# An attention and expert kernel: counts two places behind their comparisons, a step budget for routing, and query and value loads in exchanged places

## The chip, the cores and the metric

The program runs on one core of a Trainium2 chip. The metric is the device time of one execution in microseconds (us); lower is better. Engines are called as in the profile: PE (TensorE), DVE (VectorE), ACT (ScalarE), POOL (GpSimd) and SP (SyncE, which here only issues transfers).

## What is computed

Attention over 4 batches of 8 heads, 768 positions of 64 numbers, in which a position sees the first 8 positions and the last 96, with a bias that falls with distance. Its output, 3072 tokens of 512 numbers, goes to a mixture of 8 experts: each token goes to its best expert, and each expert keeps the 80 tokens with the largest gate.

```python
scores = scale * np.matmul(q, k.transpose(0, 1, 3, 2)) + bias
a = softmax(where(keep, scores, -1e9)); attn = np.matmul(a, v)
x = attn.transpose(0, 2, 1, 3).reshape(B * S, H * D)
expert_idx = np.argmax(x @ w_gate, axis=1)
for e in range(E):
    tok_idx = the (at most 80) tokens of expert e with the largest gate
    out[tok_idx] = gate_w[tok_idx, None] * (np.maximum(x[tok_idx] @ w1[e], 0) @ w2[e])
```

## The kernel before

**Rounds.** The attention runs in 24 rounds (t = 0 to 23), one block of 128 queries with all 8 heads in each; a round has two units a_ = 2t and b_ = 2t + 1 of four heads. What stands in a round is written out by hand and every engine runs its instructions in that order. A round holds work of several blocks: the second half of the values' products of block t-3 (`own`, L321), the scores of block t (`scores`, L173), the softmax of its two units (`soft`: L190 on DVE, L194 on ACT), the transposes of the probabilities of block t-1 (`transposes`, L227 to L240 on PE; one half of the result is copied by ACT, L244, the other by DVE in `copied`, L250), the first half of the values' products of block t-2 (`common`, L306), the division of the probabilities by their sums (`norm`: L201 and L202 on DVE, then L207 on POOL), and small products for the gate (`logits1`, `logits2`). The transposes write to PSUM tiles that must have been copied out before the next transposes start.

**Routing.** Blocks are gathered in groups of 6, 6, 6, 4 and 2. When the gate's numbers of a group are there, the choice of experts runs as a Python generator whose steps, one or two instructions each, are strewn into later rounds: `routes(4)` stands in the middle of a round (behind the transposes of unit b_ - 2 and ahead of their DVE copy), `routes(5)` at its end. I call these the middle and the end place. For a group of six the steps are: seven for the largest gate (`all`), for the first group alone those of a scale, then `choose` with its comparisons (L582, one per block, 127 columns each, on DVE), two empty steps, `count` (L639: six pairs of a weight load and a small matmul on PE that read the comparisons), one more empty step, and then the finish: the capacity's subtraction (L573), two steps on `re` (L599, L600), two for the gate (L608, L609) and eight on POOL (`columns`, L619 to L626). An empty step costs one of the four or five and nothing else. The first three groups finish inside the rounds, so their counts stand at the end of rounds 11, 16 and 22.

**Loads.** SP issues all transfers in one order. In a round it stores two pieces of attention output (L253; each waits for the DVE copy of its unit), loads the values of block t+1 and a piece of the next batch's keys behind the first store, and the queries of block t+2 and, in some rounds, 512 KB of expert weights (L90) or of zeros (L94) behind the second. Each transfer also waits for the one eight places ahead of it. Queries and values have four buffers each. The values of a block are first read two rounds after its scores.

**Behind the rounds** come a drain, in which the last units and the last two groups follow a written order (`DRAIN`, where `r` is one routing step), the search for each expert's threshold, and the experts.

Of the kernel before, what the change touches and what calls it, by code (L numbers as in the profile page):

```python
# [15 lines left out]
ALU = mybir.AluOpType  # L16
# [8 lines left out]
NT = B * NB  # L25
# [35 lines left out]
STAY = (3, 0)  # L61
SPLIT = (4, 4, 4)
FAR = 1.0e6
END = object()
SLOPES = [2.0 ** -(h + 1) for h in range(H)]


def fast_path(tc, a, out, cst, x_dram, inp):
    nc = tc.nc
    V, A, G, T = nc.vector, nc.scalar, nc.gpsimd, nc.tensor  # L70
    ident = cst["ident"]

    with ExitStack() as ctx:
# [63 lines left out]
        with tc.tile_pool(name="at_sb", bufs=2) as sp, ExitStack() as sctx:  # L137
# [255 lines left out]
                for _ in islice(g, n):  # L393
                    pass

            def routes(n):
                for _ in range(n):
                    while routing and next(routing[0], END) is END:
                        routing.pop(0)

            routing, cst["later"], cst["landed"] = [], [], []
            nu = 2 * NT
# [8 lines left out]
            for t in range(NT):  # L411
                a_, b_ = 2 * t, 2 * t + 1
                if t % NB == 1 and t // NB + 1 < B:
                    keys = inp.keys(t // NB + 1)
                if t == 0:
                    for _ in cst["first"]:
                        pass
                begin(a_)
                begin(b_)
                if 3 <= t:  # L420
                    own(t - 3)
                scores(a_)
                scores(b_)
                if t:
                    norm(b_ - 2)
                soft(a_, (0,))
                if t:
                    transposes(a_ - 2)
                soft(a_, (1,))
                soft(b_, (0,))  # L430
                if t:
                    copied(a_ - 2)
                if 2 <= t < NT - 1:
                    inp.load_v(t + 1)
                keys = keys if keys and next(keys, END) is not END else None
                soft(b_, (1,))
                if t % 2 == 0 and 4 <= t:
                    logits1(t - 4, 2)
                if t % 2 and 5 <= t:
                    logits2(t - 5, 2)  # L440
                norm(a_)
                if t == 0:
                    for _ in window:
                        pass
                    for z in pwz:
                        G.memset(z[:, 4 * WH:], 0.0)
                    G.memset(cst["zero"], 0.0)
                if t:
                    for _ in range(6):
                        next(late, None)  # L450
                if 2 <= t:
                    common(t - 2)
                if t:
                    transposes(b_ - 2)
                routes(4)
                if t:
                    copied(b_ - 2)
                if 1 <= t < NT - 2:
                    inp.load_q(t + 2)
                for k in ASKS[t]:  # L460
                    next(dict(w=ahead, o=wipe).get(k, iter(())), None)
                routes(5)
# [29 lines left out]
            go(choice, 99)  # L492
            cn = lps[:, 3 * P + 2 * E:3 * P + 3 * E]
            count(nc, cn, [rt])
            routes(99)
            assert not routing
            go(end, 1)
            gs1 = cst["gs1"]
# [14 lines left out]
class Route:  # L513
# [36 lines left out]
    def scale(self, ps):  # L550

        V, n, scl = self.nc.vector, self.n, self.cst["scl"]
        c = 1.0 / (STEPS * n * P)
# [1 line left out]
        mb = self.sp.tile([P, 1], BF16, name="mb", bufs=1)  # L555
        yield V.tensor_reduce(out=ms, in_=self.sx, axis=AX.X, op=ALU.add)
        yield V.tensor_scalar(out=mb, in0=ms, scalar1=-c, scalar2=float(E) * n * c, op0=ALU.mult, op1=ALU.add)
        yield
        yield
        self.nc.tensor.matmul(ps, self.cst["ones"], mb, start=True, stop=True, skip_group_check=True)  # L560
        yield V.tensor_scalar(out=scl[:, 0:1], in0=ps, scalar1=1.0 / 32, scalar2=None, op0=ALU.mult)
        kv = self.cst["kval1"]
# [2 lines left out]

    def rest(self, cn, capm):
        yield from self.choose()
        yield
        yield
        count(self.nc, cn, [self])  # L570
        if capm is not None:
            yield
            yield self.nc.vector.tensor_tensor(out=capm[:P - 1], in0=capm[:P - 1], in1=cn[:P - 1], op=ALU.subtract)  # L573
        yield from self.finish()

    def choose(self):
# [13 lines left out]
        if self.ones:  # L590
            yield V.tensor_reduce(out=self.m2, in_=eq, axis=AX.X, op=ALU.max)
        yield V.tensor_tensor(out=oh, in0=eq, in1=self.wide(self.m2), op=ALU.is_equal)
        m = 1 if self.t0 + n < NT - 5 else 2
        for t in range(n - 1 if self.ones else 0, n, m):
            yield compare(t, min(m, n - t))

    def finish(self):
        V, re = self.nc.vector, self.re
# [13 lines left out]
    def columns(self):  # L612


        G, oh, n = self.nc.gpsimd, self.oh, self.n
        c = [self.bx[:, :, i, :] for i in range(6)]
        og = self.cst["og"][:, self.t0:self.t0 + n]
        tv = self.cst["tval"][:, self.t0:self.t0 + n]
        yield G.tensor_tensor(out=og, in0=oh, in1=self.wide(self.gate), op=ALU.mult)  # L619
        yield G.tensor_copy(out=c[3], in_=og)  # L620
        yield G.tensor_tensor(out=c[0], in0=oh, in1=self.wide(tv), op=ALU.mult)
        yield G.tensor_tensor(out=og, in0=og, in1=c[3], op=ALU.subtract)
        yield G.tensor_copy(out=c[4], in_=og)
        yield G.tensor_tensor(out=c[1], in0=oh, in1=self.cst["pval"].unsqueeze(1).broadcast_to([P, n, E]), op=ALU.mult)
        yield G.tensor_tensor(out=c[5], in0=og, in1=c[4], op=ALU.subtract)
        yield G.tensor_copy(out=c[2], in_=oh)  # L626


# [812 lines left out]
```

## Time and profile before

| | us |
|---|---|
| median of three runs | 284.09 |
| lowest and highest of them | 281.59, 286.69 |
| the profiled execution's own time | 282.35 |
| its span from first to last instruction | 280.5 |
| of the span: the 24 rounds up to the last scores' start | 146 |
| the drain and the search | 146 to 178 |
| the experts | 178 to 280.5 |

Busy shares over the whole span are PE 89%, DVE 81%, ACT 73%, POOL 48%. A busy share averages over stages, so the rounds are read one by one in the timeline: which engine's row has an idle time in brackets, and what ended it.

### The profile page before, as it was taken

To read this page: it belongs to the slowest core of one execution; us is meant where nothing else is said; L and a number is where in the kernel's file an instruction comes from. 1 tells how busy PE (TensorE), PEld (TensorE's weight loads), DVE (VectorE), ACT (ScalarE), POOL (GpSimd) and SP (SyncE) were. 2 spreads that over 40 slices of the span, in tenths; PEclk is the share of its full clock that TensorE was granted. 3 is DMA by queue.
4 is the path that set the end of the run, shared out by engine and by line. 5 is a ranking of instruction groups with operands and counts; after the bars stand their busy time and mean duration, and the time that the engine had idled before them with its cause. 6 is when DMAs were issued, how large, how long until landed. Compare 5 with 4: busy or idle time off the path is not lost. (4 is left out here: it accounts for less than half of the span.)

```text
span 280.5 us, 9657 instructions
## 1 busy us (share of the span) xinstructions
PE 248.6 (89%) x3585; PEld 184.2 (66%) x3585; DVE 227.9 (81%) x785; ACT 204.6 (73%) x583; POOL 134.2 (48%) x203
## 2 busy tenths in 40 slices
PE   6769989997995969979878988999999999999990
PEld 2457868875884859767767774556666666666660
DVE  4968768899676887937966777989999999999960
ACT  4888879986686757857856455678798887989730
POOL 7585656443373242734334143880826537173431
PEclk9999999999899888979989975999999999999997
DMA  6999999967779799999861069799999999990001
GB/s 175 315 275 362 271 285 318 329 202 221 201 212 293 208 308 370 301 345 303 237 230 48 17 231 361 238 316 333 398 395 381 397 315 403 349 370 24 23 27 29
DMA packets 48030, 73.06 MB, mean 260 GB/s; under 512 B 3656, under 2 KB 22472, under 8 KB 47976
## 3 DMA queue, kind: packets, MB, share of 16 engines
q1 hardware_dynamic: 46808, 69.74, 76.3%
q0 software_dynamic: 1024, 2.62, 3.0%
q8 instruction: 30, 0.49, 0.7%
q14 instruction: 24, 0.20, 0.2%
q10 hardware_dynamic: 144, 0.00, 0.0%
HBM read 58.46 MB, written 13.89 MB: 258 GB/s over the span
## 5 line engine op out<-in xcount | busy, mean ns | idle before, releaser
L207 POOL TENSOR_TENSOR pwz<-pwz,z 128x672 f32<-128x672 f32 (+2 forms) x48 | 60.6, 1262 | 74.8 <-DVE z L202 22.0
L194 ACT ACTIVATE pwz<-ts,nm 128x168 f32<-128x168 f32 (+1 forms) x192 | 80.0, 420 | 20.2 <-DVE nm L190 17.6
L190 DVE CUSTOM_DVE_ANT_0 ts<-sc,tab 128x168 f32<-128x168 f32 (+1 forms) x192 | 50.6, 319 | 13.8 <-PE sc L173 13.3
L852 POOL TENSOR_TENSOR w_3l<-w,w_3h 128x1024 fp32r<-128x1024 f32 x7 | 26.8, 3828 | 37.9 <-issue 24.2
L173 PE MATMUL sc<-kt,q 64*64 64x104 f32 (+3 forms) x1088 | 37.5, 279 | 7.1 <-DMA q<-in_q_dram 6.1
L173 PEld LDWEIGHTS sc<-kt,q 64*64 64x64 f32 x1088 | 32.1, 142 | 10.7 <-DMA q<-in_q_dram 5.6
L194 ACT ACTIVATION_READ_ACCUMULATOR pwz<-ts,nm 128x1 f32 x192 | 36.3, 189 | 0.0
L250 DVE COPY ta<-tp 128x512 f32<-128x512 f32 (+2 forms) x47 | 28.6, 609 | 3.8 <-PE tp L240 2.9
L852 DVE TENSOR_TENSOR w_0l<-w,w_0h 128x1024 fp32r<-128x1024 f32 x15 | 30.3, 2019 | 1.5 <-ACT w_0h L847 1.1
L227 PE MATMUL tp<-ident,pwz 64*128 64x64 f32 x384 | 24.7, 239 | 5.7 <-ACT ta L244 2.6
L244 ACT COPY ta<-tp 128x512 f32<-128x512 f32 (+2 forms) x47 | 23.9, 508 | 5.4 <-PE tp L240 3.1
L227 PEld LDWEIGHTS tp<-ident,pwz 64*128 64x128 f32 x384 | 17.3, 141 | 14.8 <-POOL pwz L207 5.1
L306 PE MATMUL u<-ta,va 104*64 104x128 f32 (+1 forms) x352 | 25.4, 287 | 0.0
L321 PE MATMUL u<-ta,vb 64*64 64x64 f32 x608 | 24.3, 236 | 0.0
L306 PEld LDWEIGHTS u<-ta,va 104*64 104x64 f32 (+1 forms) x352 | 19.9, 142 | 6.3 <-PE tp L240 2.5
L321 PEld LDWEIGHTS u<-ta,vb 64*64 64x64 f32 x608 | 21.5, 148 | 1.3 <-issue 0.2
L852 DVE TENSOR_TENSOR w_1l<-w,w_1h 128x1024 fp32r<-128x1024 f32 x15 | 20.4, 1358 | 0.0
L921 POOL DMA_INDIRECT out_dram<-vb,si x8 | 13.8, 1720 | 12.0 <-ACT vb L920 6.8
L852 DVE TENSOR_TENSOR w_2l<-w,w_2h 128x1024 fp32r<-128x1024 f32 x15 | 18.1, 1209 | 0.0
L847 ACT CAST w_3h<-w 128x1024 fp32r<-128x1024 f32 x16 | 16.7, 1045 | 0.0
L847 ACT CAST w_2h<-w 128x1024 fp32r<-128x1024 f32 x15 | 15.8, 1056 | 1.2 <-PE hp L878 1.2
L190 DVE DVE_READ_ACCUMULATOR2_ANT nm<- 128x1 f32 x192 | 15.9, 83 | 0.0
(431 smaller groups left out, 548.0 us busy)
## 6 DMA issues: line engine op xcount, KB each, us to landing
w<-in_w_dram SPq DMA_DIRECT2D x64, 512.0 KB
out_dram<-zero SPq DMA_DIRECT2D x12, 512.0 KB
q<-in_q_dram SPq DMA_DIRECT2D x23, 256.0 KB
kt<-in_kT_dram SPq DMA_DIRECT2D x20, 272.0 KB
vb<-in_vb_dram SPq DMA_DIRECT2D x20, 256.0 KB
va<-in_va_dram SPq DMA_DIRECT2D x20, 208.0 KB
x_dram<-ta SPq DMA_DIRECT2D x28, 128.0 KB
x_dram<-kt SPq DMA_DIRECT2D x6, 256.0 KB
```

The lines of the kernel that those rows point to most:

```text
L173: T.matmul(sc[64 * i:64 * i + 64, hh, pp, o:o + e - c], q[h, pr * P + 64 * i:pr * P + 64 * i + 64], kt[h, pr, c0 + c:c0 + e], start=True, ...
L190: V.tensor_tensor_reduce(out=ts[:, j, :w], in0=sc[:, hh, pp, :w], in1=cst["tab" if m else "tab0"][:, 2 * g + pp, hh, :], scale=-0.125, sca ...
L194: A.activation(out=pw[:, j, :w], in_=ts[:, j, :w], func=AF.Exp, bias=nm[:, j:j + 1], scale=-1.0, accum_out=z[:, j:j + 1],)
L207: eng.tensor_tensor(out=p, in0=p, in1=zs.unsqueeze(2).broadcast_to(list(p.shape)), op=ALU.mult)
L227: T.transpose(out=tps[i][:, 64 * j:64 * j + 64], in_=pw[hs[i], o:o + P], identity=ident[hs[i], hs[i]])
L244: A.copy(out=ta[:, 0, :n], in_=tps[0][:, :n])
L250: V.tensor_copy(out=ta[:, 1, :n], in_=tp[:, :n])
L306: T.matmul(up[64 * hh:64 * hh + 64, pr, :], va[:n, 64 * h:64 * h + 64], ta[:n, :, 64 * j:64 * j + 64], start=pr == 0, stop=not m, skip_gro ...
L321: T.matmul(up[h, pr, 64 * i:64 * i + 64], vb[h, i, pr, :], ta[h, i, 256 + 64 * pp:320 + 64 * pp], start=False, stop=True, skip_group_check ...
L847: A.copy(out=hi, in_=src)
L852: eng.tensor_tensor(out=lo, in0=src, in1=hi, op=ALU.subtract)
L921: G.indirect_dma_start(out=out[:, :], out_offset=bass.IndirectOffsetOnAxis(ap=si[:, e:e + 1], axis=0), in_=y, in_offset=None, bounds_check ...
```

## The change

Five things are edited. (1) The places' numbers become a budget: an ordinary step costs 1, a comparison costs 3 (`SLOW`), and a `HOLD` ends the place, so that the two holds ahead of a count put it two places behind the last comparison. The middle place has 5 instead of 4. (2) All comparisons take two blocks in one instruction of 254 columns; before, those of the first three groups took one of 127. (3) POOL's eight steps are put into five yields. (4) `load_q(t + 2)` moves to where `load_v(t + 1)` stood, and the reverse. (5) At the end of the drain the remaining steps run without regard to holds.

```diff
-            def routes(n):
-                for _ in range(n):
-                    while routing and next(routing[0], END) is END:
+            def routes(n, hold=True):
+                while n > 0 and routing:
+                    step = next(routing[0], END)
+                    if step is END:
                         routing.pop(0)
+                    elif step is HOLD and hold:
+                        break
+                    else:
+                        n -= 3 if step is SLOW else 1
...
-                if 2 <= t < NT - 1:
-                    inp.load_v(t + 1)
+                if 1 <= t < NT - 2:
+                    inp.load_q(t + 2)
...
-                routes(4)
+                routes(5)
                 if t:
                     copied(b_ - 2)
-                if 1 <= t < NT - 2:
-                    inp.load_q(t + 2)
+                if 2 <= t < NT - 1:
+                    inp.load_v(t + 1)
...
         yield from self.choose()
-        yield
-        yield
+        yield HOLD
+        yield HOLD
         count(self.nc, cn, [self])
         if capm is not None:
-            yield
+            yield HOLD
...
-        m = 1 if self.t0 + n < NT - 5 else 2
-        for t in range(n - 1 if self.ones else 0, n, m):
-            yield compare(t, min(m, n - t))
+        for t in range(n - 1 if self.ones else 0, n, 2):
+            compare(t, min(2, n - t))
+            yield SLOW
```

On PE, the end of round 16 in the program before: the transposes of unit 31 end with L240, then comes the count of the third group (six such pairs; one stands here), then `own` of block 14 and the scores of round 17.

```order
L240 MATMUL tp_31_2293<-ident,ut_1242 128x64
L639 LDWEIGHTS cf_2178
L639 MATMUL lps<-oh,cf_2178 127x8
...
L321 MATMUL u_2283<-ta_2094,vb_118 64x64 x8
L321 MATMUL u_2283<-ta_2147,vb_118 64x64 x8
L173 MATMUL sc_2351<-kt_113,q_110 64x104
```

The same place of the changed program, and then the end of round 17, where the count now stands (`cf` are the comparisons' results):

```order
L240 MATMUL tp_31_2289<-ident,ut_1242 128x64
L321 MATMUL u_2279<-ta_2091,vb_118 64x64 x8
L321 MATMUL u_2279<-ta_2143,vb_118 64x64 x8
L173 MATMUL sc_2338<-kt_113,q_110 64x104
...
L240 MATMUL tp_33_2430<-ident,ut_1242 128x64
L644 LDWEIGHTS cf_2175
L644 MATMUL lps<-oh,cf_2175 127x8
...
L321 MATMUL u_2420<-ta_2236,vb_119 64x64 x8
```

So the count has moved by one round, past `own` of block 14, the scores of round 17 and that round's transposes.

On DVE, the middle and end place of round 16 before, from the reciprocal of unit 32's sums to the first softmax rows of round 17:

```order
L202 RECIPROCAL z_2182<-z_2182 128x4
L582 TENSOR_TENSOR cf_2178<-sx_1599,kval_65 128x127 x4
L250 COPY ta_2294<-tp_31_2293 128x512
L582 TENSOR_TENSOR cf_2178<-sx_1599,kval_65 128x127
L573 TENSOR_TENSOR capm<-capm,lps 127x8
L201 TENSOR_SCALAR z_2185<-z_2185 128x4
L202 RECIPROCAL z_2185<-z_2185 128x4
L190 ISA ts_2329,nm_2327<-sc_2351,tab 128x168
```

and the same stretch after the change:

```order
L202 RECIPROCAL z_2179<-z_2179 128x4
L587 TENSOR_TENSOR cf_2175<-sx_1597,kval_65 128x254 x2
L250 COPY ta_2290<-tp_31_2289 128x512
L201 TENSOR_SCALAR z_2182<-z_2182 128x4
L202 RECIPROCAL z_2182<-z_2182 128x4
L190 ISA ts_2316,nm_2314<-sc_2338,tab 128x168
```

Two comparisons of two blocks stand where four and one of one block stood, and the subtraction L573 has gone to the middle place of round 18, together with the four instructions of the finish:

```order
L202 RECIPROCAL z_2461<-z_2461 128x4
L578 TENSOR_TENSOR capm<-capm,lps 127x8
L604 TENSOR_SCALAR re<-oh 128x48
L605 TENSOR_TENSOR re<-re,sx_1597 128x48
L613 TENSOR_SCALAR sx_1597<-sx_1597 128x6
L614 RECIPROCAL gate<-sx_1597 128x6
L250 COPY ta_2572<-tp_35_2571 128x512
```

On SP, round 13 before; `q_112` is the buffer of block 15's queries:

```order
L253 DMA x_dram<-ta_1847 256x1x128
L1361 DMA va<-in_va_dram 104x512
L1362 DMA vb_118<-in_vb_dram 128x512
L1346 DMA kt_114<-in_kT_dram 128x4x136
L253 DMA x_dram<-ta_1896 256x1x128
L1354 DMA q_112<-in_q_dram 128x512
L90 DMA w_0_0_1914<-in_w_dram 128x2x512
```

and after:

```order
L253 DMA x_dram<-ta_1832 256x1x128
L1359 DMA q_112<-in_q_dram 128x512
L1351 DMA kt_114<-in_kT_dram 128x4x136
L253 DMA x_dram<-ta_1880 256x1x128
L1366 DMA va<-in_va_dram 104x512
L1367 DMA vb_118<-in_vb_dram 128x512
L90 DMA w_0_0_1903<-in_w_dram 128x2x512
```

The query load stands four places earlier, behind one store instead of two. Weight loads that the diff doesn't name have moved as well: at the end of round 16 three stood in a row before, and now rounds 15, 16 and 17 have them one at a time.

## Rows read from the trace of the kernel before

**Rows 1.** Stretches: us, busy us of each engine, PE clock, DMA share, GB/s.
```profile
103.60:106.90 3.30, 3.30 (x67) 3.30 (x68) 0.50 (x4) 0.58 (x1) 1.31 (x1) 0.50 1.12 338
107.00:116.50 9.50, 9.50 (x239) 8.02 (x232) 9.28 (x49) 8.44 (x35) 4.12 (x8) 1.00 1.04 356
178.00:280.00 102.00, 95.61 (x476) 62.93 (x476) 91.74 (x88) 77.53 (x101) 47.72 (x21) 0.99 0.77 272
```

**Rows 2.** Who waited for whom: total us, times, longest us; PE.
```profile
PE sc L173 <- DMA q<-in_q_dram: 6.1, 6, 2.9
PE lps L639 <- DVE cf L582: 5.2, 8, 1.1
...
PE lps L350 <- issue: 2.1, 1, 2.1
```

**Rows 3.** Timeline, rounds 16 and 17: start, us, engine, what [idle before].
```profile
100.63 1.97 DVE L582 TENSOR_TENSOR cf<-sx,kval 128x127 bf16<-128x127 f32 x4
...
102.45 0.42 PE L639 MATMUL lps<-oh,cf 128*127 128x8 bf16 x2 [1.09 <-DVE cf L582]
102.52 0.68 DVE L250 COPY ta<-tp 128x512 f32<-128x512 f32 x1
...
103.60 1.97 PE L321 MATMUL u<-ta,vb 64*64 64x64 f32 x32
...
106.83 0.33 DVE L190 CUSTOM_DVE_ANT_0 ts<-sc,tab 128x168 f32<-128x168 f32 x1 [2.66 <-PE sc L173]
```

**Rows 4.** Timeline, the same products and scores at the full clock, rounds 18, 19.
```profile
115.52 1.15 PE L321 MATMUL u<-ta,vb 64*64 64x64 f32 x32
...
116.51 1.41 PE L173 MATMUL sc<-kt,q 64*64 64x104 f32 x48
```

**Rows 5.** Timeline, first softmax row of rounds 12 and 23.
```profile
72.75 0.29 DVE L190 CUSTOM_DVE_ANT_0 ts<-sc,tab 128x128 f32<-128x128 f32 x1 [1.85 <-PE sc L173]
...
147.73 0.29 DVE L190 CUSTOM_DVE_ANT_0 ts<-sc,tab 128x128 f32<-128x128 f32 x1 [2.34 <-PE sc L173]
```

**Rows 6.** Timeline, rounds 13 to 15: SP's issues, PE, DVE and ACT.
```profile
80.06 0.54 SPq L253 DMA_DIRECT2D x_dram<-ta  x1
80.69 1.73 SPq L1361 DMA_DIRECT2D va<-in_va_dram  x1
...
84.25 0.60 SPq L1354 DMA_DIRECT2D q<-in_q_dram  x1
...
86.02 0.29 PE L240 MATMUL tp<-ident,ut 64*128 64x64 f32 x4
...
89.21 2.04 PE L173 MATMUL sc<-kt,q 64*64 64x104 f32 x48 [2.90 <-DMA q<-in_q_dram]
90.16 0.33 DVE L190 CUSTOM_DVE_ANT_0 ts<-sc,tab 128x168 f32<-128x168 f32 x1 [2.21 <-PE sc L173]
...
92.32 0.58 ACT L244 COPY ta<-tp 128x512 f32<-128x512 f32 x1 [0.78 <-PE tp L240]
```

**Rows 7.** Timeline, scores of rounds 21 and 22.
```profile
131.30 1.43 PE L173 MATMUL sc<-kt,q 64*64 64x104 f32 x48 [0.51 <-DMA q<-in_q_dram]
...
137.28 1.46 PE L173 MATMUL sc<-kt,q 64*64 64x104 f32 x48 [0.80 <-DMA q<-in_q_dram]
```

**Rows 8.** One line's instructions: ns min/median/max, first and last start us, forms.
```profile
L582 DVE TENSOR_TENSOR cf<-sx,kval x18: 258/282/1396, 63.8 to 144.3; 128x127 bf16<-128x127 f32 x18
L582 DVE TENSOR_TENSOR cf<-tail,kval x4: 284/355/416, 157.9 to 161.1; 128x254 bf16<-128x254 f32 x2, 128x127 bf16<-128x127 f32 x2
...
L608 DVE TENSOR_SCALAR sx<-sx x3: 140/893/1156, 75.7 to 151.2; 128x6 f32<-128x6 f32 x3
```

**Rows 9.** Timeline: POOL's division in round 16, and four counts without a wait.
```profile
100.88 1.37 POOL L207 TENSOR_TENSOR pwz<-pwz,z 128x672 f32<-128x672 f32 x1 [1.91 <-DVE cf L582]
...
159.88 0.38 PE L639 MATMUL lps<-oh,cf 128*127 128x8 bf16 x4
```

**Rows 10.** Timeline, round 19: a stall on PE.
```profile
120.67 0.58 PE L350 MATMUL lps<-ident,ls 128*128 128x128 f32 x2 [2.11 <-issue]
```

More of the change, by code (lines that the diff above doesn't have):

```diff
@@ L63 @@
 FAR = 1.0e6
-END = object()
+END, HOLD, SLOW = object(), object(), object()
 SLOPES = [2.0 ** -(h + 1) for h in range(H)]
@@ L494, in fast_path @@
             count(nc, cn, [rt])
-            routes(99)
+            routes(99, False)
             assert not routing
@@ L567, in rest @@
         yield from self.choose()
-        yield
-        yield
+        yield HOLD
+        yield HOLD
         count(self.nc, cn, [self])
         if capm is not None:
-            yield
+            yield HOLD
             yield self.nc.vector.tensor_tensor(out=capm[:P - 1], in0=capm[:P - 1], in1=cn[:P - 1], op=ALU.subtract)
@@ L618, in columns @@
         tv = self.cst["tval"][:, self.t0:self.t0 + n]
-        yield G.tensor_tensor(out=og, in0=oh, in1=self.wide(self.gate), op=ALU.mult)
+        G.tensor_tensor(out=og, in0=oh, in1=self.wide(self.gate), op=ALU.mult)
         yield G.tensor_copy(out=c[3], in_=og)
-        yield G.tensor_tensor(out=c[0], in0=oh, in1=self.wide(tv), op=ALU.mult)
+        G.tensor_tensor(out=c[0], in0=oh, in1=self.wide(tv), op=ALU.mult)
         yield G.tensor_tensor(out=og, in0=og, in1=c[3], op=ALU.subtract)
-        yield G.tensor_copy(out=c[4], in_=og)
+        G.tensor_copy(out=c[4], in_=og)
         yield G.tensor_tensor(out=c[1], in0=oh, in1=self.cst["pval"].unsqueeze(1).broadcast_to([P, n, E]), op=ALU.mult)
-        yield G.tensor_tensor(out=c[5], in0=og, in1=c[4], op=ALU.subtract)
+        G.tensor_tensor(out=c[5], in0=og, in1=c[4], op=ALU.subtract)
         yield G.tensor_copy(out=c[2], in_=oh)
```

## The prediction

> **What bounds the kernel now.** I read the stretches first [rows 1]. In the experts' 102 us PE is busy for 95.6, and nothing in the change touches them, so that part stays. In an undisturbed stretch, 107.0 to 116.5, PE is busy for all 9.50 us at a granted clock of 1.00, with DVE at 9.28 and ACT at 8.44. So a round, about 6 us from one block's scores at 131.30 to the next at 137.28 [rows 7], is paced by PE, with the two others close behind. What a round can lose is therefore a wait of PE, and the list of waits names them [rows 2]: PE waited 6.1 us in six places for queries, 5.2 us in eight places for comparisons, and 2.1 us once for nothing that the profile shows.
>
> The timeline shows what such a wait really costs [rows 3]. In round 16 DVE starts the third group's comparisons at 100.63, PE stands in the count behind them, and only at 103.60 come the products of block 14. They take 1.97 us where the same 32 take 1.15 two rounds later [rows 4], because the granted clock of 103.6 to 106.9 is 0.50, the 1.2 GHz level, after PE had stood still [rows 1]. DVE meanwhile is done with the round and waits 2.66 us for the scores, until 106.83. That idle time, not PE's, is what the stall costs: DVE's next round, and ACT's behind it, start that much late. The other two counts inside the rounds show the same, 1.85 us in front of round 12's softmax and 2.34 us in front of round 23's [rows 5].
>
> The second kind is the queries of block 15 [rows 6]. SP issues their load at 84.25; PE has finished round 14 at 86.02 + 0.29 = 86.31 and waits 2.90 us, until 89.21. DVE waits 2.21 us for the scores, and ACT another 0.78 us for PE in the slow stretch that follows.
>
> **Part by part: the counts.** With the count one round later, its comparisons have been done for a whole round, so its waits go. In round 16 PE can then follow its last transposes with the products (1.15 us) and the scores (1.41 us) [rows 4], about 2.6 us, and be done by 103; DVE's copy ends at 102.52 + 0.68 = 103.20 [rows 3]. So the scores no longer end last, and DVE sets the pace: its idle time goes, 2.66 + 1.85 + 2.34 = 6.85 us. In rounds 16 and 22 one comparison (0.28) stood behind the copy; pairing takes it out of that place: 0.56. Together 7.4 us.
>
> The comparisons themselves: five or six of 0.28 us become three of at most 0.42 [rows 8]. But the longest took 1396 ns, since POOL's division, from 100.88 for 1.37 us, runs at that moment [rows 9]. If one of each pair still meets it, DVE's middle place is about as long as before (1.39 + 0.42 against 1.97), a gain of nothing; if none does, it is 1.0 us shorter in three rounds. I take nothing, as the collision came in every group. The Trainium skill, "SBUF — State Buffer", section "Who interferes with whom", says that a DVE instruction with two SBUF inputs contends with a GpSimd instruction that reads SBUF, and that whoever starts first holds the port pair for its whole instruction. The trace agrees with its 1396 ns. By that rule a longer comparison is as exposed as a short one, and the sum is the one with nothing.
>
> What the move costs: a count is six pairs, and four took 0.38 us unhindered [rows 9], so 0.57 us. In rounds 12, 17 and 23 they now lie in a round that PE paces (9.50 of 9.50): three times 0.57 is 1.7 us lost. From below nothing, should DVE pace these rounds too; I take 1.7. The finish moves a round later, its five instructions in one middle place ahead of DVE's copy. Its `sx` step took 140 ns at its shortest and 1156 where POOL ran [rows 8]; in round 13 it now stands later behind the reciprocal that releases POOL, so it probably collides. That is between 0 and 1.0 us; DVE's spare time is small, 0.22 us of 9.50 [rows 1], but the copy that it delays has the next scores of PE, 1.41 us, as cover, so I take 0.5. POOL's steps keep their number and POOL is the least busy engine [rows 1]: hidden, as long as its 1.37 us division isn't late.
>
> **The loads.** The query load of round 13 goes from behind the values, keys and second store to right behind the first store: it can issue at 80.6 rather than 84.25 [rows 6]. Before, it landed 89.21 - 84.25 = 4.96 us after its issue. SP's next issue at 80.69 was held for 1.73 us, and the query load would now meet that hold: landing between 85.6 and 87.3, against 86.31 when PE wants it. The wait of 2.90 shrinks to between 0 and 1.0, and with a wait this short the clock need not fall. Gain: 2.21 + 0.78 = 3.0 us, or 2.0 at the poor end. The waits in rounds 21 and 22 were 0.51 and 0.80 [rows 7]; earlier loads take both away, and I count the first alone, since in round 22 DVE has a group's choice to do at that moment: 0.5. The values are read two rounds after the scores, so half a round's delay lies inside about 12 us of cover (two rounds of 6 us). If that cover were gone, each late load would cost PE what the queries' did, 2 to 3 us. The single weight loads in place of three in a row, the drain's shifted steps and the last group's count behind two transposed blocks I set at nothing: they are hidden by PE's queue of products, and at most the 0.38 us of four counts comes onto the path.
>
> **The sum**: 7.4 + 3.0 + 0.5 - 1.7 - 0.5 = 8.7 us off the profiled execution's 282.35: 273.6, and I say 274. That execution lies 1.7 us below the median of 284.09; the runs' spread of 5.1 us is the size of two such stalls, so I leave the difference in the range.
>
> **The rivals.**
>
> *More*: no comparison of a pair meets POOL, and the waits of rounds 21 and 22 both count: 1.0 us in three rounds and 0.8 on top, 274 - 3.8 = 270. Against it stands that each group had one collision; for it, that fewer instructions are exposed.
>
> *The wait moves*: DVE, 9.28 us busy of 9.50 [rows 1], is late all the same, and PE now waits for its copies of the transposes instead of its comparisons. Half of the 7.4 us stays: 277.5.
>
> *The loads do nothing*: the hold of 1.73 us, not the place in the order, sets when queries land, because the transfers are full (DMA share 1.04 and 356 GB/s [rows 1]). Then 3.5 us is missing: 277.
>
> *Slower*: PE's unexplained stall in round 19, 2.11 us at 120.67 [rows 10], comes oftener. It is a wait for nothing that the profile shows, which fits a late load of PE's own instructions behind other transfers; the stretch before it moved 356 GB/s at a DMA share of 1.04. Rounds without other waits move the same bytes in less time. One such stall costs 2.1 us and a slow clock after it (1.97 for 1.15 us on each group of products), about 3 us. Three more cancel the gain, four make it slower than 284, five or six slower by 2%. The Trainium skill, "Runtime: NRT & Kernel Launch", section "Instruction fetch mechanics", says that crossing from one block of instructions to the next is mostly hidden. By that rule this rival is worth nothing; the trace has one wait that it doesn't explain.
>
> **How the numbers follow.** I give the forecast, 271.5 to 276, 0.46; more 0.11; the wait moves 0.20; the loads do nothing 0.12; slower 0.11. A measurement of this kernel tells about 2% from no change: that is 278.4 on the fast side and 289.8 on the slow. Faster by more are the forecast and "more" whole, half of the moved wait (0.10) and 0.07 of the loads: 0.74. Slower by more is 0.05 of the last rival. Within 2% is the rest, 0.21. The range is 268.5 (all of "more", and most of the 1.7 us of the counts hidden after all) to 281 (both partial rivals at once: 282.35 less 8.7 - 3.7 - 3.5); beyond it I leave the last rival and a tail of the first.
>
> **What would show it.** Right: no wait of PE for comparisons inside the rounds; DVE's idle time in front of the first softmax of rounds 12, 17 and 23 under 0.5 us; the scores of block 15 without a wait of over 1 us; the granted clock at 1.00 at the end of round 16, where it was 0.50; the experts still 102 us. The comparisons of 254 columns should show one of about 1.4 us in a group. Wrong: a wait of PE's transposes for DVE's copy of about 1 us in each of rounds 12, 17 and 23 (the wait has moved); the queries' waits still there (the loads do nothing); several waits of PE for nothing shown (slower). If the time is out by more than 5 us, the step to doubt is that DVE's idle time can be taken off whole: that nothing else than PE's count held the next round.

## The result and the profile after

| | before | changed |
|---|---|---|
| median, us | 283.91 | 273.11 |
| lowest and highest of four runs | 281.59, 286.69 | 271.25, 274.21 |
| profiled execution's own time | 282.35 | 272.51 |
| its span | 280.5 | 270.7 |
| start of the scores of round 9 | 50.33 | 50.35 |
| from there to the start of the scores of round 23 | 96.05 | 85.10 |
| from there to the end | 134.13 | 135.22 |

The changed kernel is faster: ratio 0.9639, 95% interval 0.9548 to 0.973. The prediction was 274.0 us, 268.5 to 281.0, and 8.7 us off the profiled execution; it was 9.84 off. The table shows where: rounds 9 to 22 got 10.95 us shorter and what follows 1.09 us longer. A round's length is taken here from the first score product (L173) of its block to that of the next, read from the timeline:

| round | before | changed | difference | what stood there |
|---|---|---|---|---|
| 11, 16, 22 | 8.97, 9.65, 9.10 | 6.03, 5.92, 6.36 | -9.41 | the counts |
| 12, 17 | 5.65, 5.78 | 5.82, 6.32 | +0.71 | where two of the counts went |
| 14, 15 | 7.23, 6.50 | 4.42, 6.01 | -3.30 | the queries of block 15 |
| 19 | 8.87 | 5.98 | -2.89 | the stall of [rows 10] |
| 10, 18 | 6.68, 5.37 | 8.11, 7.05 | +3.11 | new stalls, below |
| 9, 13, 20, 21 | 22.26 | 23.07 | +0.81 | |

Lines of the kernel from the counts on are five higher than before: L582 is now L587, L639 is L644, L573 is L578.

Stretches of the changed kernel, the answer to [rows 1] (us, busy us of each engine with the number of instructions, PE clock, DMA share, GB/s): all of rounds 9 to 22, the end of round 16 with round 17, and the experts. Behind them stands the first of these stretches in the kernel before.

```profile
50.35:135.45 85.10, 76.16 (x1812) 63.36 (x1810) 74.05 (x375) 69.86 (x277) 40.98 (x56) 0.98 0.96 299
97.00:106.80 9.80, 9.52 (x237) 7.80 (x233) 8.71 (x43) 8.49 (x33) 5.23 (x4) 1.00 1.05 331
165.40:267.40 102.00, 98.14 (x489) 64.10 (x487) 94.13 (x90) 77.90 (x102) 50.22 (x22) 1.00 0.77 274
```

```profile
50.33:146.38 96.05, 82.58 (x1818) 69.11 (x1817) 76.31 (x388) 70.44 (x277) 42.26 (x57) 0.92 0.87 266
```

The last of the three is 102 us long by choice. From the experts' first product (L878, now L883) to the end it is 102.52 us before and 102.35 after, so the experts take what they took.

PE does the same work (some 1,810 products) and waits less: 85.10 - 76.16 = 8.9 us idle where it was 96.05 - 82.58 = 13.5. It also needs 6.4 us less busy time, since the granted clock has a mean of 0.98 instead of 0.92. At the end of round 16 it is 1.00, where it was 0.50. The same bytes now go through in 85 us: 299 GB/s and a DMA share of 0.96 instead of 266 and 0.87.

Who waited for whom in the changed kernel, PE, the answer to [rows 2]:

```profile
PE u L306 <- issue: 3.6, 3, 1.7
PE sc L173 <- DMA q<-in_q_dram: 2.8, 5, 1.0
...
PE sc L173 <- issue: 1.6, 2, 0.9
...
PE lps L644 <- DVE oh L597: 0.4, 1, 0.4
```

No wait of PE for comparisons (`cf`) is left, queries cost 2.8 us where it was 6.1, and the first place has a wait for "issue", nothing that the profile shows. No product waits for the values, whose loads now issue later.

Timeline of rounds 16 and 17, the answer to [rows 3] (start, us, engine, what, [idle before]):

```profile
96.59 1.15 PE L321 MATMUL u<-ta,vb 64*64 64x64 f32 x32
...
96.94 1.84 DVE L587 TENSOR_TENSOR cf<-sx,kval 128x254 bf16<-128x254 f32 x2
97.20 1.31 POOL L207 TENSOR_TENSOR pwz<-pwz,z 128x672 f32<-128x672 f32 x1 [1.91 <-DVE z L202]
97.58 1.41 PE L173 MATMUL sc<-kt,q 64*64 64x104 f32 x48
98.71 0.68 DVE L250 COPY ta<-tp 128x512 f32<-128x512 f32 x1
...
99.59 0.30 DVE L190 CUSTOM_DVE_ANT_0 ts<-sc,tab 128x168 f32<-128x168 f32 x1
...
102.52 0.46 PE L644 MATMUL lps<-oh,cf 128*127 128x8 bf16 x6
...
102.91 1.15 PE L321 MATMUL u<-ta,vb 64*64 64x64 f32 x32
```

At 96.59 PE goes on with the products of block 14 at once, in 1.15 us instead of 1.97. DVE's two comparisons run beside the scores, and its first softmax row at 99.59 has no idle time in brackets, where [rows 3] had 2.66 us. The count stands at 102.52, one round later, without a wait. Rounds 12 and 23 begin on DVE in the same way, for 1.85 and 2.34 us in [rows 5]:

```profile
71.59 0.26 DVE L190 CUSTOM_DVE_ANT_0 ts<-sc,tab 128x128 f32<-128x128 f32 x1
...
136.89 0.26 DVE L190 CUSTOM_DVE_ANT_0 ts<-sc,tab 128x128 f32<-128x128 f32 x1
```

### The profile page after: what moved, and what is told of

Its sections match the earlier page's. It is cut to its first block, busy times and chain, and to the rows that moved or that the text cites. A ratio compares the mean times of both kernels' runs of the same rounds, so it can differ in the third digit from the quotient of the medians.

```text
span 270.7 us, 9646 instructions
## 1 busy us (share of the span) xinstructions
PE 243.4 (90%) x3585; PEld 179.4 (66%) x3585; DVE 226.9 (84%) x776; ACT 204.5 (76%) x583; POOL 133.7 (49%) x203
## 5 line engine op out<-in xcount | busy, mean ns | idle before, releaser
L173 PE MATMUL sc<-kt,q 64*64 64x104 f32 (+3 forms) x1088 | 36.0, 271 | 4.3 <-DMA q<-in_q_dram 2.8
L173 PEld LDWEIGHTS sc<-kt,q 64*64 64x64 f32 x1088 | 30.7, 137 | 7.7 <-issue 3.9
L306 PEld LDWEIGHTS u<-ta,va 104*64 104x64 f32 (+1 forms) x352 | 19.1, 136 | 10.6 <-issue 6.9
L321 PE MATMUL u<-ta,vb 64*64 64x64 f32 x608 | 22.2, 224 | 0.0
L321 PEld LDWEIGHTS u<-ta,vb 64*64 64x64 f32 x608 | 19.6, 137 | 1.6 <-DMA x_dram<-ta 0.6
```

What stands on the lines that cost most here:

```text
L173: T.matmul(sc[64 * i:64 * i + 64, hh, pp, o:o + e - c], q[h, pr * P + 64 * i:pr * P + 64 * i + 64], kt[h, pr, c0 + c:c0 + e], start=True, ...
L306: T.matmul(up[64 * hh:64 * hh + 64, pr, :], va[:n, 64 * h:64 * h + 64], ta[:n, :, 64 * j:64 * j + 64], start=pr == 0, stop=not m, skip_gro ...
L321: T.matmul(up[h, pr, 64 * i:64 * i + 64], vb[h, i, pr, :], ta[h, i, 256 + 64 * pp:320 + 64 * pp], start=False, stop=True, skip_group_check ...
```

## The experiments

**The loads alone.** The kernel before, with `load_q` and `load_v` exchanged.

```diff
-                if 2 <= t < NT - 1:
-                    inp.load_v(t + 1)
+                if 1 <= t < NT - 2:
+                    inp.load_q(t + 2)
...
-                if 1 <= t < NT - 2:
-                    inp.load_q(t + 2)
+                if 2 <= t < NT - 1:
+                    inp.load_v(t + 1)
```

> The kernel before with nothing but the two loads in each other's place. Theory (the wait for queries was 3.5 us of the time): PE's wait for queries in front of the scores of block 15, 2.90 us before, is under 1 us, the waits for comparisons stay as they were (5.2 us in eight places), and the time is 3 to 3.5 us below the kernel before, about 279 against 282.35 in the profiled executions. Rival (the loads do nothing, full transfers set when queries land): the sum of PE's waits for queries stays near 6 us and the time is within 1 us of before.

Measured: 278.36 us against 282.87 of the kernel before on the same chip, ratio 0.9832 (0.9769 to 0.9895), so 3.0 to 6.5 us; by the medians 4.5, more than the 3 to 3.5 expected. PE's waits in it:

```profile
PE lps L639 <- DVE cf L582: 4.8, 7, 1.1
...
PE u L306 <- issue: 1.9, 1, 1.9
PE tp L240 <- issue: 1.7, 1, 1.7
PE sc L173 <- DMA q<-in_q_dram: 1.6, 3, 1.0
```

The comparisons' waits are there as before, the queries' have gone from 6.1 to 1.6. "The loads do nothing" has fallen. The two waits for issue are new, with a third of 1.2 us that isn't shown, and that of L350 [rows 10] is gone.

**The counts alone.** The changed kernel with the two loads back in their old places (the diff above, reversed).

> The changed kernel with the two loads back where they stood; counts, budget and pairs as changed. Theory (the three stalls at the counts cost 7.4 us, and 2.2 us of it is given back): about 277 in the profiled execution; no wait of PE for comparisons in the rounds, DVE's idle time ahead of rounds 12, 17 and 23 under 0.5 us, but the wait for the queries of block 15 still 2 to 3 us. From the round lengths of the changed kernel, which show nothing given back in rounds 12 and 17, it would rather be 274 to 275. Rival (the loads did the work): 280 or more.

Measured: 275.27, ratio 0.9696 (0.9625 to 0.9768), 6.6 to 10.6 us. PE waits for no comparison, and for the queries of block 15 it does (timeline):

```profile
86.08 0.29 PE L240 MATMUL tp<-ident,ut 64*128 64x64 f32 x4
88.42 0.85 PE L173 MATMUL sc<-kt,q 64*64 64x104 f32 x23 [2.05 <-DMA q<-in_q_dram]
```

So both parts pay by themselves. Their sum, 4.5 + 7.6 = 12.1 us by the medians, is not to be told, within these intervals, from the whole change's 10.8.

**No holds.** The changed kernel in which a hold is an empty step. This takes the first group's `scale` its two holds as well, which the change had put there too.

```diff
-                    elif step is HOLD and hold:
+                    elif step is HOLD and hold is None:
```

> The changed kernel in which a hold is an ordinary empty step and ends no place; budget, pairs and loads as changed. The counts then stand at the ends of rounds 11, 16 and 22 again, where they stood before, but with one or two paired comparisons in the same round's middle place instead of four or five single ones. Theory (the place of the count is what matters): PE waits for comparisons again, 0.4 to 1.1 us in each of these rounds, and 3 to 6 us come back: 276 to 278. Rival (fewer comparisons between the transposes and the count are enough): no wait over 0.3 us and a time within 1 us of the changed kernel's 272.5.

Measured: 273.88, ratio 0.9597 (0.9507 to 0.9687), not to be told from the changed kernel. The trace shows more. Timeline at the end of round 16, PE and then DVE:

```profile
96.95 0.28 PE L644 MATMUL lps<-oh,cf 128*127 128x8 bf16 x2 [0.37 <-DVE cf L587]
98.40 0.28 PE L644 MATMUL lps<-oh,cf 128*127 128x8 bf16 x2 [1.17 <-DVE cf L587]
...
100.95 0.33 DVE L190 CUSTOM_DVE_ANT_0 ts<-sc,tab 128x168 f32<-128x168 f32 x1 [1.55 <-PE sc L173]
```

Rounds 16 and 22, with two pairs ahead of the count, have the stall back (8.65 and 9.19 us long, against 5.92 and 6.36 with holds). Round 11, with one pair, has not (6.28 against 6.03). Rounds 9 to 22 take 89.07 us, 3 to 4 more than in the changed kernel's two traces (85.10, and 85.95 below), as expected. But from round 23 to the end it takes 133.86, 1.2 to 1.4 less. So the holds are what clears rounds 16 and 22, and about a third of what the rounds gain is paid back behind them. The theory's 3 to 6 us was right for the rounds and too much for the whole.

**One block a comparison.** The changed kernel, each pair made as two.

```diff
-            compare(t, min(2, n - t))
+            for i in range(t, min(t + 2, n)):
+                compare(i, 1)
```

> The changed kernel with each comparison of two blocks made as two of one block in the same step, so that places and budget stay. Theory (pairing is worth nothing by itself, one of each group meets POOL either way): the time stays within 0.5 us of the changed kernel's 272.5 in the profiled execution, and one comparison in each group still takes about 1.4 us. Rival (the longer instructions are what makes the middle place shorter): 0.3 to 1.0 us in each of three rounds, so 273.5 to 275.5.

Measured: 273.01, ratio 0.9645 (0.9561 to 0.9729), not to be told from the changed kernel; an effect of 1 us would not show in these intervals. The profiled execution, 273.77 us, is 1.3 above the changed kernel's, which by the expectation speaks for the rival. The rounds say otherwise: rounds 12, 16 and 17 are 0.14 to 0.15 us longer than in the changed kernel's second trace (below) and round 11 not at all, while round 21 alone has 10.24 us for 6.21 in the first trace, with a wait for issue of 2.4 us in it. One comparison in each group still takes 1.40 us. So pairing shows no effect of the size of the rival's.

**What the waits for issue are.** The changed kernel stops in round 10 and again in round 18 (timeline, PE), and a transfer of the queue "instruction" runs just before the first (transfers from 58.3 to 60.1):

```profile
58.76 0.98 PE L306 MATMUL u<-ta,va 104*64 104x128 f32 x13
...
61.39 0.44 PE L306 MATMUL u<-ta,va 104*64 104x128 f32 x3 [1.66 <-issue]
...
63.88 2.52 PE L173 MATMUL sc<-kt,q 64*64 64x104 f32 x48
```

```profile
108.41 0.98 PE L306 MATMUL u<-ta,va 104*64 104x128 f32 x13 [1.53 <-issue]
```

```profile
q8 instruction: 1, 0.02, 4.4%
```

PE stops inside a row of sixteen equal products, and the scores behind run at the slow clock: 2.52 us for 1.41, and the stretches give 0.50 from 63.1 to 66.4:

```profile
63.10:66.40 3.30, 3.30 (x70) 3.11 (x68) 2.30 (x16) 1.22 (x5) 1.31 (x1) 0.50 0.79 254
```

The trace has 30 transfers of 16 KB on that queue, for some 7,270 instructions of PE, which are 28.4 times 256. The one here began at 58.70 and took 1.27 us, and PE went on 1.42 us after its end. I numbered PE's instructions from the start of the trace (weight loads, products, semaphore waits and a few others): the first one late in round 10 has number 2241, in round 18 it has 4289, and in the kernel before the stall of [rows 10] has 4545. These are 8, 16 and 17 times 256, plus 193. A third stop, 1.04 us in round 22, has 20 x 256 + 193, though the waits put it down to ACT. The Trainium skill, "Runtime: NRT & Kernel Launch", section "Instruction fetch mechanics", says that instructions are refilled in blocks of 256, 16 KiB each; the trace agrees in the size of the transfers and in the spacing of the stops. To test it, the changed kernel was run again, and then with transfers moved.

> The changed kernel as it is, as the base of the three others of this batch. Expected 271 to 274. If PE's waits for nothing shown are late loads of its own instructions, they stand at the same places of PE's instruction stream as before: counting weight loads, matmuls and semaphore waits from the start of the trace, after a multiple of 256 plus 193, so that the 1.66 us in round 10 comes again at instruction 2241; if they are something else, they stand anywhere.

Measured: 270.95, ratio 0.9628 (0.957 to 0.9686). The stop at 2241 came again (1.38 us), and every stop of 0.5 us and more in rounds 9 to 22 stands at such a number. Stops of 0.6 us and more in rounds 9 to 22 that stand at a multiple of 256 plus 193, by instruction number (from the end of any earlier PE instruction to the next, so a little less than the bracket of [rows 10]), in every trace; the orders of the drain and the moved transfers are those of the runs further down:

| kernel | stops, us |
|---|---|
| before | 4545: 2.04 |
| changed | 2241: 1.66; 4289: 1.53; 5313: 1.04 |
| changed, again | 2241: 1.38; 4289: 1.45; 4801: 1.56; 5057: 1.85; 5313: 1.10 |
| the loads alone | 2241: 1.94; 4801: 1.66; 5313: 1.08 |
| the counts alone | 2241: 1.69; 5313: 0.75 |
| no holds | 2241: 1.60; 3009: 0.98; 4801: 1.27; 5057: 1.11; 5313: 0.75 |
| one block a comparison | 2241: 1.38; 4289: 1.24; 4545: 1.63; 4801: 0.67; 5057: 2.39 |
| first drain order | 2241: 1.39; 3009: 0.97; 4289: 2.00; 4801: 1.22; 5057: 1.02 |
| second drain order | 4289: 1.99; 4801: 1.63; 5057: 1.57; 5313: 0.82 |
| one weight load moved | 2241: 1.66; 4289: 1.54; 4801: 2.77 |
| zeros moved, first drain order | 2241: 1.11; 4289: 1.72 |
| zeros moved, second drain order | 2241: 1.05; 4289: 1.82 |
| zeros and 3 weight loads moved | 1985: 0.80; 2753: 0.82; 3777: 0.65; 4033: 1.52; 4289: 0.99; 4545: 2.06 |
| zeros and 9 weight loads moved | none (2753: 0.54) |

All 46 of these stops end 1.2 to 1.7 us after the end of a 16 KB transfer of that queue. In the run without them the transfers also begin earlier: between 4289 and 5569 each begins when PE is 8 to 50 instructions past the last of these numbers, in the changed kernel 102 to 173 past it. So by these numbers the stops are PE waiting for instructions whose transfer came late, though the trace doesn't say which instructions a transfer holds.

**The drain.** From round 23 to the end the kernels with the holds take 135.05 to 135.5 us, those without 133.4 to 134.1. What follows the drain varies by up to 1 us too, so the drain alone, from the start of the last scores to the first product of the search (L704, now L709), tells more: 15.58 us before, 14.96 with the loads alone and 15.63 without holds, but 16.38 to 16.99 in the four traces with holds and the same order of the drain (16.47 and 16.81 in the changed kernel's two). Timeline of PE at the drain's end in the changed kernel, and in the kernel before (see also the four counts in [rows 9]):

```profile
148.95 1.07 PE L106 MATMUL xp<-ident,ut 128*128 128x128 f32 x8
150.44 0.76 PE L644 MATMUL lps<-oh,cf 128*127 128x8 bf16 x6 [0.41 <-DVE oh L597]
151.92 0.19 PE L709 MATMUL jb<-gs,ones 128*128 128x8 bf16 x1 [0.73 <-DVE gs L504]
```

```profile
161.19 0.51 PE L639 MATMUL lps<-oh,cf 128*127 128x8 bf16 x2
161.96 0.18 PE L704 MATMUL jb<-gs,ones 128*128 128x8 bf16 x1 [0.26 <-DVE gs L499]
```

The finish of the third group, a round later, has used up the drain's steps; the fourth group's count falls behind the transposed blocks (L106), and the search waits for it. First I added six steps (`r`) early in the drain:

```diff
-    "r w44 r a1 r r n47 r r t46 a2 r r r r w45 r r r "
+    "r r w44 r r a1 r r r r n47 r r r t46 a2 r r r r w45 r r r "
```

> The changed kernel with six more routing steps early in the drain, so that the fourth group's count stands ahead of the last two transposed blocks again, as in the kernel before. Theory (from the start of the last scores to the end the changed kernel takes 1.1 us more than the kernel before, since the third group's finish, a round later, pushes the fourth group's count behind those blocks): the threshold search starts 0.8 to 1.1 us earlier and the time falls by as much, to 271.5 in a profiled execution. Rival (the drain is only slower because the clock falls earlier): no more than 0.3 us.

Measured: 271.27, ratio 0.9657 (0.9599 to 0.9716): no gain. The wait of L709 is 0.26 us again, but the third group's steps on POOL now stand ahead of POOL's last division, and PE waits for that (timeline); from round 23 to the end it is 136.0 us, and the drain alone takes 17.12.

```profile
147.17 0.46 PE L227 MATMUL tp<-ident,pwz 64*128 64x64 f32 x8 [0.81 <-POOL pwz L207]
```

With the steps at the very start of the drain:

```diff
+    "r r r r r r r w44 r r a1 r r n47 r r t46 a2 r r r r w45 r r r "
```

> The changed kernel with the extra routing steps put at the very start of the drain, so that the third group's steps on POOL end before POOL's last division; in the earlier drain run they stood ahead of it and PE waited 0.81 us for that division. Theory (the two orders together are the drain's loss: 0.5 us of it is the third group's count, the rest these steps): from the start of the last scores to the end 134.3 to 134.7 us, against 135.2 and 135.1 of the changed kernel's two profiles and 134.1 of the kernel before. Rival: 135.0 or more again, and the loss has yet another cause.

Measured: a median of 271.76 us of four from 267.60 to 273.39, so the whole time tells nothing. From round 23 to the end it is 134.64 us, as expected, in a profiled execution of 270.74; the drain alone takes 16.19, and 16.25 in the three later runs with this order. So the place of the steps was part of the loss. The 0.6 us that remain against 15.58 and 15.63 are near the size of the third group's count, 0.51 us on PE's path in round 23; that they are this count is not shown by a run of its own.

**Transfers moved out of the rounds.** First one weight load of 512 KB from round 9 to round 10 (`ASKS` says in which round a `w` or an `o`, six stores of zeros, is issued), on top of the first drain order:

```diff
-ASKS = "- - - w w w w w w w - w - w - w - o o o o o o -".split()
+ASKS = "- - - w w w w w w - w w - w - w - o o o o o o -".split()
```

> As the run before it, and one 512 KB weight load moved from the end of round 9 to the end of round 10. Theory (PE's stop of 1.66 us in round 10 is an instruction load that waits in the transfer queues, and the weight load of round 9 is what fills them): the stop in round 10 is gone or under 0.5 us, and with it the slow clock behind it, 1.5 to 3 us less than without the move. Rival (the stop has to do with PE's own work there): it stays at 1.4 to 1.9 us.

Measured: 270.76, ratio 0.9663 (0.9598 to 0.9728), and the stop in round 10 is still 1.66 us: this expectation missed. Then, instead, the six stores of zeros moved into the drain (a new drain step `o` is `next(wipe)`):

```diff
-ASKS = "- - - w w w w w w w - w - w - w - o o o o o o -".split()
+ASKS = "- - - w w w w w w w - w - w - w - - - - - - - -".split()
...
+    "r r o w44 r r o a1 r r r r o n47 r r r o t46 a2 r r r r o w45 r r r o "
```

> As the drain run, and the six 512 KB stores of zeros moved from rounds 17 to 22 to behind the last attention stores in the drain, where the transfers move 79 GB/s. Theory (instructions come late because the transfers of the rounds are full): the stops of PE for nothing shown after round 16 (1.53 us in round 18 and 1.04 in round 22 of the changed kernel) are gone, the one in round 10 stays, and the time is 1.5 to 3 us less than with the drain alone. Rival (the stores don't matter): the stops after round 16 stay, 2 us or more together. A third outcome: the drain's own stores wait behind the zeros, and what the rounds gain the drain loses.

Measured: 270.32, ratio 0.9614 (0.9537 to 0.9692). The stops behind round 18 are gone (table), the one at 4289, in round 18, isn't, against the theory. In the trace the last scores start at 130.36, 4.8 us earlier than with the drain order alone (135.18); the median, of six executions from 266.92 to 274.83, shows less.

Next, with the zeros so and the second drain order, the weight loads of rounds 7 to 9 moved behind round 9:

```diff
+ASKS = "- - - w w w w - - - w w w w w w - - - - - - - -".split()
...
+    "r r r r r o r r o w44 r r o a1 r r o n47 r r t46 o a2 r r r r o w45 r r r "
```

> As the run before it, with the six stores of zeros in the drain and the weight loads of rounds 7, 8 and 9 later, one a round in rounds 10 to 15. Theory (PE's stops for nothing shown are instruction loads that wait behind full transfers): the stop in round 10 (instruction 2241), which one weight load less in round 9 didn't take away, goes under 0.5 us with three less; those after round 17 stay away, as with the zeros moved; other stops may come where the weights now are (rounds 11 to 16). Rival (it is something in the instructions there): 1.1 us or more at instruction 2241, as in all runs with the changed routing.

Measured: 270.98, ratio 0.9556 (0.9495 to 0.9617). The profiled execution, 273.75 us, was the longest of its six, so its rounds (87.61 us for 9 to 22) are no measure of this kernel. Its stops are in the table: none at 2241 and others in rounds 12 and 16, where the weights now are, both as expected, but also two behind round 17 (4289 and 4545), where none was expected. The next run has the same loads up to round 14. In it the six weight loads that stood outside the written order are in the drain too (`w` is `next(ahead)`):

```diff
+    "r r r r r o r r o w44 w r r o w a1 r r o w n47 r r w t46 o w a2 r r r r o w w45 r r r "
```

> As the run before it, and also the six weight loads that stood in rounds 15 to 19 outside the written order, in the drain between the zeros. Theory: the stop at instruction 4289 (round 18, 1.72 us even with the zeros moved) goes under 0.5 us, rounds 16 to 22 take 5 to 6 us each, and the last scores start about 129; the drain and the search, which now carry 6 MB more, may be 0 to 3 us longer, so the whole is 264 to 268. Rival: the stop stays, and so does round 18 at 7 us.

Measured: 274.53, ratio 0.9699 (0.9643 to 0.9756). Stretch of rounds 9 to 22, PE's waits for issue, and the timeline at the first expert:

```profile
48.84:128.70 79.86, 75.18 (x1812) 62.29 (x1811) 72.94 (x375) 68.75 (x274) 40.17 (x51) 1.00 0.81 245
```

```profile
PE u L306 <- issue: 0.8, 2, 0.5
PE cnt L731 <- issue: 0.6, 1, 0.6
PE sc L173 <- issue: 0.2, 1, 0.2
```

```profile
158.50 2.94 SPq L94 DMA_DIRECT2D out_dram<-zero  x3
...
166.43 1.17 PE L948 MATMUL lps<-w_0l,early 128*128 128x480 f32 x2 [6.59 <-DVE w_0l L857]
```

With 245 GB/s instead of 299 no stop of 0.6 us is left in these rounds, the clock is 1.00 throughout, and rounds 9 to 22 take 79.86 us instead of 85.10 and 85.95. (That round 10 has no stop proves little by itself: with the second drain order alone and all transfers in place there was none of 0.6 us either.) The last scores start at 128.70, as expected. But the whole is 3.6 us slower than the run before: the experts wait 6.59 us for DVE, DVE for POOL, and POOL for stores of attention output that SP issues behind the moved transfers. From round 23 to the end it takes 144.2 us; here the expectation, 0 to 3 us more, missed. Last, only the zeros moved (`ASKS` as in the run with the zeros alone), with the second drain order:

> The two moves that paid, together: the six stores of zeros in the drain (all weight loads where the changed kernel has them) and the third group's steps at the start of the drain. Theory: the last scores start at 130 to 131, as in the earlier run with the zeros in the drain, and 134.6 follow, so about 265 in a profiled execution, 1.5 to 2% below the changed kernel's 270.7 and 269.9. Rival (instruction loads come late at random, and the zeros only shift where): stops of PE of 5 us or more together in the rounds and 268 or more.

Measured: 269.49, ratio 0.9569 (0.9519 to 0.9619), the lowest median of all; its interval still overlaps the changed kernel's. The last scores start at 133.04, later than expected, with the stops at 2241 (1.05 us) and 4289 (1.82), and the profiled execution took 269.29 us where about 265 was expected. Its stops sum to 2.9 us, less than the rival's 5, and its time is the rival's: neither came out whole.

## Why the prediction was right, step by step

**Counts: right, under-sized.** DVE's idle times went as said: no wait of PE for comparisons, none of DVE ahead of rounds 12, 17 and 23, the clock at 1.00. Expected were 7.4 us, the three rounds got 9.41 shorter, most of the difference in round 11 (2.94 for 1.85), though the changed round 11 begins in a slow stretch of its own; in the second trace, without that stretch, it takes 4.90 us, 4.07 less than before. The prediction took only DVE's idle time off this round. Before, PE also waited there for ACT's copy (timeline), and in the changed kernel it doesn't; what else there is stays open.

```profile
66.69 0.73 PE L227 MATMUL tp<-ident,pwz 64*128 64x64 f32 x8 [0.72 <-ACT ta L244]
```

"The wait moves" fell: the longest wait of PE's transposes for DVE's copy in rounds 12 and 17 is this (timeline), 0.25 us where about 1 would have shown it.

```profile
99.44 0.46 PE L227 MATMUL tp<-ident,pwz 64*128 64x64 f32 x7 [0.25 <-DVE ta L250]
```

**Comparisons: right.** One line's instructions in the changed kernel (ns min/median/max), the answer to [rows 8]:

```profile
L587 DVE TENSOR_TENSOR cf<-sx,kval x9: 392/415/1530, 63.7 to 134.6; 128x254 bf16<-128x254 f32 x9
```

```profile
L613 DVE TENSOR_SCALAR sx<-sx x3: 171/172/172, 81.3 to 144.4; 128x6 f32<-128x6 f32 x3
```

A long one is still there in each group, 1529 or 1530 ns, beside POOL's division (the two at 96.94 take 1.84 us together), so pairing won nothing that shows, and the run with single blocks bears that out. The `sx` step (L613) did not collide: the 0.5 us set for it were not paid.

**What the move costs: right in size, partly in another place.** Of the 1.7 us for the counts in PE-paced rounds, 0.71 shows in rounds 12 and 17, and the third count's 0.51 lies in round 23. The drain's shifted steps were "set at nothing", at most 0.38: this step failed. The drain alone got 0.89 us longer (16.47 for 15.58), 0.4 more than the count, and an order that makes room takes back 0.2 to 0.3 of it (16.19 and 16.25), 0.6 in the second trace. The granted clock was 1.00 through the changed kernel's drain, so a slow clock is not the cause there.

**Loads: right.** The queries of block 15 (timeline, SP and PE), the answer to [rows 6]:

```profile
79.35 0.60 SPq L1359 DMA_DIRECT2D q<-in_q_dram  x1
...
85.43 0.29 PE L240 MATMUL tp<-ident,ut 64*128 64x64 f32 x4
85.65 1.46 PE L173 MATMUL sc<-kt,q 64*64 64x104 f32 x48
```

The load issues at 79.35, the scores wait for nothing, and rounds 14 and 15 gained 3.30 us for 3.0. The 0.5 us for rounds 21 and 22 failed: in this trace their waits stayed, 0.53 and 0.95 us for [rows 7]'s 0.51 and 0.80. In the second trace PE waits for no queries in the rounds, but stops at 5057 and 5313 in those two.

```profile
122.88 1.37 PE L173 MATMUL sc<-kt,q 64*64 64x104 f32 x44 [0.53 <-DMA q<-in_q_dram]
```

```profile
129.09 1.46 PE L173 MATMUL sc<-kt,q 64*64 64x104 f32 x48 [0.95 <-DMA q<-in_q_dram]
```

**The stall of [rows 10]: half seen.** The "slower" rival said that late instruction loads would come oftener, since the same bytes go through in less time. They did: one stop of 0.6 us in the trace before, three and five in the changed kernel's two. Its mechanism was right and its price wrong. It set some 3 us for each; rounds 10 and 18 got 1.43 and 1.68 us longer with stops of 1.66 and 1.53. Three more were to cancel the gain of 8.7 us, yet the execution with four more took 271.71 us, where the median before was 281.61 on that chip. At most the stops cost the difference to the run without them, 5 to 6 us in rounds 9 to 22 (85.10 and 85.95 against 79.86); that run also carries less data there, and the 1.9 us that the changed kernel's first trace waits for queries in these rounds are gone in it too.

**Why the sum came near.** Partly by luck, since terms that were off cancel. The three rounds of the counts gave 2.0 us more than 7.4, the loads 0.3 more than 3.0, the counts' places cost 0.5 less than 1.7, and the 0.5 of `sx` was not paid. Against it stand the 0.5 of rounds 21 and 22 that did not come, 0.6 us behind the count in what follows the start of round 23, 0.8 us in rounds 9, 13, 20 and 21, and 0.2 net of stops (+3.11 - 2.89). Together that is 1.2, and 9.84 - 8.7 is 1.1.

## What to carry to other kernels

Where an engine that sets the pace reads results made just ahead of it, put a whole stage between the two, and then look at what the moved steps push out behind the loop. When waits go, the same transfers run in less time: look next at what shares their queues, PE's own instructions among it. A wait for nothing that the profile shows, in the middle of a row of equal products, is worth counting: stops that stand multiples of 256 instructions apart went with late instruction loads here. Taking 6 MB of transfers out of the stretch, with three more moved inside it, left only a short one; moving one inside it left them, and the time won was lost again where the transfers went.

## What the runs showed of the hardware

PE's instructions came in transfers of 16 KB on a queue of their own, whose time the profile counts among the same 16 transfer engines as the data's. At 292 and 299 GB/s in rounds 9 to 22 (the changed kernel's two traces) several of them in an execution came late, each time with a stop; all stops of 0.6 to 2.8 us at these numbers ended 1.2 to 1.7 us after such a transfer, for instance at 2241, 4289 and, in the kernel before, 4545 (ends 59.97, 106.82 and 119.17, next instruction at 61.39, 108.41 and 120.67). At 245 GB/s only one was left, of 0.54 us. The mean rate doesn't decide alone: two were left at 277 and at 271 GB/s with the zeros moved, and six at 259 with three weight loads moved as well. The Trainium skill, "Runtime: NRT & Kernel Launch", section "Instruction fetch mechanics", says that crossing a block is mostly hidden; here the measurement decides: at a DMA share of 0.93 and 0.96 it was not. Which loads are late differs between executions of one kernel: the table's second and third row are the same program.
